# Half 0 of batch 0's tokens first in the planner's list, and a third scratch slot for narrowing

## The chip, the cores and the metric

One core of one Trainium2 chip. The time is device microseconds of one execution, the median of several runs. TensorE is PE below, VectorE DVE, ScalarE ACT, GpSimd POOL, and SyncE, which issues nearly all transfers, SP.

## What is computed

Nyström attention over 4 batches of 8 heads, 576 tokens and 64 columns per head, then two feed-forward layers over the 2304 tokens.

```python
def _attn_ref(q, k, v):
    m = 32                                   # landmarks: means of 18 tokens
    q_lm = q.reshape(B, H, m, S // m, D).mean(axis=3)
    k_lm = k.reshape(B, H, m, S // m, D).mean(axis=3)
    A, Bm, C = sm(q, k_lm), sm(q_lm, k_lm), sm(q_lm, k)
    Z = Bm.transpose(0, 1, 3, 2) / (norm1(Bm) * norm_inf(Bm) + 1e-06)
    for _ in range(6):
        Z = 2 * Z - Z @ Bm @ Z
    return (A @ Z @ C @ v)

def _moe_ref(x, w_gate, w_val, w_out, rms_g):          # 512 -> 1536 -> 512
    xn = x / np.sqrt(np.mean(x * x, axis=-1, keepdims=True) + 1e-06) * rms_g
    g = xn @ w_gate
    return (g * (1 / (1 + np.exp(-g))) * (xn @ w_val)) @ w_out

def _moe2_ref(x, w_in, w_out, s, b):                   # 512 -> 2048 -> 512
    r = np.maximum(x @ w_in, 0.0)
    return (s * (r * r) + b) @ w_out
```

All weights of the feed-forward layers arrive as 8-byte floats and are narrowed to 4 bytes on the chip.

## The kernel before

**Order.** No engine's order is written out by hand. Every step is put on a list as an operation with a key (when it is wanted), a cost on each engine that can do it, and the names it reads and writes. A planner (`Scheduler.run`) goes through time with those costs and issues, on the engine that is free first, the ready operation with the smallest key. Attention's keys come from `by_path`: the longer the way that is left, the smaller the key. Operations of a second part of batch 0, its last half of tokens, are in `batch_late` and get 2.0 added. The costs are the planner's own; they are no measured times. Where PE would stand early on, the planner puts in fillers (`warm`, L1746): products of ones that nobody reads.

**Batch 0's end.** The tokens of a batch are worked on in two halves of 288 (half 0 and half 1). For each half: x = A'(W) on PE (L1037), the squares on ACT (L1043), half of the squares' sum on DVE (L1048), the sum over partitions on PE (L1056, twelve small products), reciprocal on DVE (L1064, L1065), root on ACT (L1068), a diagonal on DVE (L1073), a broadcast by a product with ones on PE (L1078), two scalings of A' on DVE (L1084), and then each scaled tile is split into a rounded part (`xh`, ACT L1088) and a rest (`xl`, DVE L1090). The rounded part and the rest stand for a 4-byte number in products that take 1-pass operands. After both roots ACT loads another table for the tanh (L1071).

**Narrowing** (`narrow`, L1110 on). A block of 512 KB of 8-byte weights is loaded into a stage slot, ACT writes two scratch tiles from it, `ca` (L1145) and `cmag` (L1147, and L1155, or DVE with L1156), and DVE joins the two to 4-byte weights (L1159). There are two scratch slots of each kind, and three slots `rawg` for the narrowed gate and value weights and two, `rawo`, for the narrowed output weights. A narrowed block is stored too, for the later batches.

**Products.** Hidden columns are taken in 12 slices f = 0 to 11 of 128. For a slice: the gate and value weights are multiplied with batch 0's small matrix gw (`fused`, L1299, sixteen products into two banks), the result is split into `uh` (ACT L1311 or DVE L1312) and `ul` (DVE L1314), and then, for each half of tokens and for gate and value, six products (L1326) make one bank. ACT and DVE take it from there: tanh (L1343), a product (L1345), another (L1349). Four banks, 67 to 70, serve these products, the weight products and batch 1's attention by turns. From slice 0 on the output weights follow (L1372, L1390). Batch 1's attention is laid between by the planner: its transposes on PE are L613, in triples, and its copies L617 and L618.

## Time and profile before

| | |
|---|---|
| median of 3 runs | 829.31 us (828.41 to 831.85) |
| the profiled execution | 829.26 us, of which the span 827.5 us |
| PE busy | 810.5 us (98%) |
| DVE busy | 651.0 us (79%) |
| ACT busy | 531.4 us (64%) |
| POOL busy | 119.8 us (14%) |

Busy time of PE counts fillers and includes a modelled end of each product, so two products in a row overlap; the step from one start to the next is what a product costs. Time is counted from the start of the span. The rows on which the prediction rests are shown further down.

### The profile page before, as it was taken

To read this page: it belongs to the slowest core of one execution; us is meant where nothing else is said; L and a number is where in the kernel's file an instruction comes from. 1 tells how busy PE (TensorE), PEld (TensorE's weight loads), DVE (VectorE), ACT (ScalarE), POOL (GpSimd) and SP (SyncE) were. 2 spreads that over 40 slices of the span, in tenths; PEclk is the share of its full clock that TensorE was granted. 3 is DMA by queue.
4 is the path that set the end of the run, shared out by engine and by line. 5 is a ranking of instruction groups with operands and counts; after the bars stand their busy time and mean duration, and the time that the engine had idled before them with its cause. 6 is when DMAs were issued, how large, how long until landed. Compare 5 with 4: busy or idle time off the path is not lost.

```text
span 827.5 us, 16641 instructions
## 1 busy us (share of the span) xinstructions
PE 810.5 (98%) x6151; PEld 653.3 (79%) x6151; DVE 651.0 (79%) x1461; ACT 531.4 (64%) x1097; POOL 119.8 (14%) x173
## 2 busy tenths in 40 slices
PE   8899999999999999999999999999999999999997
PEld 5577767877787877888888888887888888888886
DVE  6888998777787777898998988799766767665554
ACT  5899987543534434688888976578555556565553
POOL 0370355117411132210100000000000000000000
PEclk9999999999999999999999999999999999999999
DMA  9999959652542313398978641232422432254234
GB/s 281 326 381 368 266 178 285 222 135 81 144 139 89 128 47 125 116 295 274 321 260 316 199 169 51 90 102 70 135 77 76 112 93 80 75 164 140 64 87 130
DMA packets 87234, 138.46 MB, mean 167 GB/s; under 512 B 26480, under 2 KB 49008, under 8 KB 87152
## 3 DMA queue, kind: packets, MB, share of 16 engines
q1 hardware_dynamic: 86960, 137.13, 52.3%
q8 instruction: 48, 0.79, 0.4%
q14 instruction: 34, 0.28, 0.1%
q10 hardware_dynamic: 192, 0.26, 0.1%
HBM read 114.82 MB, written 22.54 MB: 166 GB/s over the span
## 4 chain that ended last, share of the span: by engine, by line
PE 79%; DVE 11%; ACT 5%; DMA 2%; issue 2%; POOL 0%; DVEq 0%; SPq 0%; ACTq 0%; POOLq 0%
PE bank L1417 23%; PE bank L1282 17%; PE bank L1390 14%; PE bank L1326 14%; PE bank L1664 3%; PE bank L1299 3%; PE bank L754 1%; DVE w_all L1108 1%; DVE hl L1108 1%; DVE hbuf L1345 1%; PE bank L1372 1%; ACT ca_all L1145 1%; PE bank L675 1%; DMA stage<-in_moe_w_out_dram 1%; DVE rawg L1159 1%
## 5 line engine op out<-in xcount | busy, mean ns | idle before, releaser
L1417 PE MATMUL bank<-w_all,hh 128*128 128x512 f32 x472 | 148.0, 394 | 0.0
L1390 PE MATMUL bank<-hh,w_all 128*128 128x512 f32 (+1 forms) x448 | 144.6, 379 | 0.1
L1417 PEld LDWEIGHTS bank<-w_all,hh 128*128 128x128 f32 x472 | 88.2, 188 | 20.3
L1390 PEld LDWEIGHTS bank<-hh,w_all 128*128 128x128 f32 x448 | 81.6, 188 | 24.1 <-issue 9.5
L1417 PE MATMUL bank<-w_all,hl 128*128 128x512 f32 x236 | 93.1, 394 | 0.0
L1326 PE MATMUL bank<-xh,u_all 128*128 128x288 f32 x400 | 88.2, 300 | 0.5 <-DVE hbuf L1345 0.3
L1390 PE MATMUL bank<-hl,w_all 128*128 128x512 f32 (+1 forms) x224 | 83.0, 370 | 0.0
L1108 DVE TENSOR_TENSOR w_all<-rawo,w_all 128x512 fp32r<-128x512 f32 x86 | 62.1, 722 | 12.8 <-ACT w_all L1106 10.0
L1326 PEld LDWEIGHTS bank<-xh,u_all 128*128 128x128 f32 x400 | 66.2, 188 | 4.6 <-issue 1.0
L1343 ACT ACTIVATE hbuf<-bank 128x288 f32<-128x288 f32 x96 | 38.9, 405 | 32.4 <-PE bank L1326 30.2
L1326 PE MATMUL bank<-xl,u_all 128*128 128x288 f32 x200 | 59.0, 295 | 0.2 <-DVE xl L1090 0.2
L1326 PE MATMUL bank<-xh,xl 128*128 128x288 f32 x184 | 54.2, 295 | 0.0
L1326 PE MATMUL bank<-xl,xh 128*128 128x288 f32 x184 | 54.2, 294 | 0.0
L1417 PEld LDWEIGHTS bank<-w_all,hl 128*128 128x128 f32 x236 | 44.3, 188 | 10.6
L1345 DVE SCALAR_TENSOR_TENSOR hbuf<-hbuf,bank 128x288 f32<-128x288 f32 x96 | 42.5, 443 | 8.8 <-ACT hbuf L1343 8.3
L1106 ACT ACTIVATE w_all<-rawo 128x512 fp32r<-128x512 f32 x48 | 30.3, 631 | 28.7 <-PE bank L1390 14.6
L1390 PEld LDWEIGHTS bank<-hl,w_all 128*128 128x128 f32 x224 | 42.2, 188 | 5.5 <-DVE hl L1108 0.3
L1106 ACT ACTIVATE hh<-hbuf 128x288 fp32r<-128x288 f32 (+8 forms) x73 | 26.6, 389 | 21.9 <-PE bank L1390 13.9
L1585 ACT ACTIVATE xbuf<-xbuf,b_sb,s_sb 128x512 f32<-128x512 f32 (+1 forms) x34 | 26.0, 765 | 20.2 <-DVE xbuf L1596 19.7
L1155 ACT ACTIVATE cmag_all<-stage 128x512 f16<-128x512 f32 x48 | 37.9, 790 | 1.0
L1326 PEld LDWEIGHTS bank<-xl,u_all 128*128 128x128 f32 x200 | 37.6, 188 | 1.2 <-DVE xl L1090 0.4
L1108 DVE TENSOR_TENSOR hl<-hbuf,hh 128x512 fp32r<-128x512 f32 (+8 forms) x76 | 36.9, 495 | 1.6 <-ACT hh L1106 0.2
(316 smaller groups left out, 1940.3 us busy)
## 6 DMA issues: line engine op xcount, KB each, us to landing
rawg<-keptg SPq DMA_DIRECT2D x36, 512.0 KB, 4.4
stage<-in_moe_w_out_dram SPq DMA_DIRECT2D x28, 512.0 KB, 5.5
rawo<-kepto SPq DMA_DIRECT2D x48, 256.0 KB, 3.1
rawg<-kept SPq DMA_DIRECT2D x24, 512.0 KB, 3.6
rawo<-kept SPq DMA_DIRECT2D x36, 256.0 KB, 2.6
stage<-in_moe_w_in_dram SPq DMA_DIRECT2D x16, 512.0 KB, 5.4
keptg<-rawg SPq DMA_DIRECT2D x12, 512.0 KB, 6.1
kept<-tail SPq DMA_DIRECT2D x24, 256.0 KB, 3.7
```

The source lines that it names most:

```text
L1106: e.activation(out=hi(), in_=src(), func=ACTF.Copy) if e is nc.scalar
L1108: b = op({"dve": t_dve(n), "pool": t_pool(n)}, key, lambda e: e.tensor_tensor(out=lo(), in0=src(), in1=hi().bitcast(F32), op=ALU.subtract) ...
L1155: e.activation(out=upper(), in_=word(1).bitcast(F32), func=ACTF.Copy, scale=2.0 ** -100)
L1282: nc.tensor.matmul(out=ps.t, lhsT=a[h][:, 128 * kd:128 * kd + 128], rhs=x[kd][y].t, start=(first and kd == 0 and i == 0), stop=(last and k ...
L1299: nc.tensor.matmul(out=pU[g].t[m, 256 * j:256 * j + 256], lhsT=gw[b].t[p, m], rhs=r.t[p, :, 128 * k:128 * k + 128], start=True, stop=True)
L1326: nc.tensor.matmul(out=ps.t[:, 0:HC], lhsT=u[a].t[:, 256 * g + 128 * part:256 * g + 128 * part + 128], rhs=x[y].t.rearrange("p k n -> p (k ...
L1343: op(("act", t_act(HC)), tg, lambda e: e.activation(out=th.t[:, 0:HC], in_=pg.t[:, 0:HC], func=ACTF.Tanh, scale=0.5), r=[pg], w=[th])
L1345: op(("dve", t_dve(HC)), tg, lambda e: e.scalar_tensor_tensor(out=th.t[:, 0:HC], in0=th.t[:, 0:HC], scalar=1.0, in1=pg.t[:, 0:HC], op0=ALU ...
L1390: nc.tensor.matmul(out=A[c].t[:, 0:n], lhsT=w[a].t[:, 128 * c:128 * c + 128], rhs=hs[y].t[:, 0:n], start=(f == 0 and i == 0), stop=(f == F ...
L1417: nc.tensor.matmul(out=A[c].t, lhsT=hs[a].t[:, s], rhs=w.t[:, 512 * y:512 * y + 512], start=(f == 0 and i == 0), stop=(f == F2 - 1 and i = ...
L1585: e.activation(out=h.t[:, c:c + n], in_=h.t[:, c:c + n], func=ACTF.Identity, scale=s_sb, bias=b_sb) if e is nc.scalar
L1664: nc.tensor.matmul(out=ps.t[:, 0:n], lhsT=tot.t[:, 1024 * a + c:1024 * a + c + 128], rhs=xs[3, kd // 2][y].t[:, n * (kd % 2):n * (kd % 2) ...
```

## The change

Two things, both in batch 0's end. The operations of half 0 of batch 0 that make x (`chain`: those of the loop over the halves, from the product L1037 to the split L1090, for half 0) get 8 taken off their keys, so that they come ahead of others in the planner's list. And the first three slices' gate and value weights (`f < C_F`) may be narrowed in a third scratch slot: `rawo`'s first buffer serves as `ca`, its second as `cmag`. Until the last of these operations is planned (`free_c`) the two `rawo` buffers are held back from their own use.

```diff
--- before.py
+++ after.py
@@ -37,6 +37,8 @@
 SCORE = 0.26
 BMM = 0.15
 N_SUM = 2
+CHAIN = 8
+C_F = 3
 XB = 1
 SCORE2 = 1.02
 XC = 2.0
@@ -355,7 +357,13 @@
     ro_r = ring(2, [128, 512], "rawo")
     st_r = ring(3, [128, 512], "stage", I64)
     c_all = [sb.tile([128, 1024], d, name=f"{x}_all") for x, d in (("ca", F32), ("cmag", I32))]
-    ca_r, cm_r = (Ring([Slot(x[:, 512 * i:512 * i + 512]) for i in range(2)], True) for x in c_all)
+    c_two = [[Slot(x[:, 512 * i:512 * i + 512]) for i in range(2)] for x in c_all]
+    ca_r, cm_r = (Ring(x, True) for x in c_two)
+    c_more = [Slot(ro_r.slots[0].t), Slot(ro_r.slots[1].t.bitcast(I32))]
+    ca0_r, cm0_r = (Ring(x + [y], True) for x, y in zip(c_two, c_more))
+    c_ops = []
+    for x in ro_r.slots:
+        x.held = True
     u_all = sb.tile([128, 2048], F32R, name="u_all")
     u_r = [Ring([Slot(u_all[:, 1024 * x + 512 * i:1024 * x + 512 * i + 512]) for i in range(2)], True) for x in range(2)]
     w_all = sb.tile([128, 2048], F32R, name="w_all")
@@ -491,7 +499,7 @@
 
     xs, gw = {}, {}
     at_ops = []
-    batch_ops, batch_late = {}, {}
+    batch_ops, batch_late, chain = {}, {}, []
 
     def token(b, n):
 
@@ -1095,6 +1103,8 @@
                         out=mark, in_=part(1)[:, cols][:, 0:1].bitcast(F32)), r=wl, w=["sums"])
             if hf:
                 late.extend(mine[n_mine:])
+            elif first:
+                chain.extend(mine[n_mine:])
         batch_late[b] = late
 
 
@@ -1113,7 +1123,8 @@
         c = slice(128 * f, 128 * f + 128)
         wt = ((w_gate, w_val, w_out), (w_in2, None, w_out2))[kind - 1][part]
         rows = kind == 1 and part < 2
-        st, a, m = Buf(st0_r if rows else st_r), Buf(ca_r), Buf(cm_r)
+        early = rows and f < C_F
+        st, a, m = Buf(st0_r if rows else st_r), Buf(ca0_r if early else ca_r), Buf(cm0_r if early else cm_r)
 
         def wide(x):
             return x.rearrange("p (k f) -> p k f", k=KD) if rows else x
@@ -1161,6 +1172,8 @@
             op0=ALU.logical_shift_left, op1=ALU.bitwise_or), r=[a, m, *after], w=[w], pair=True)
         if rows:
             row_ops.extend(S_.ops[n_ops:])
+        if early:
+            c_ops.extend(S_.ops[n_ops + 1:])
         for o in S_.ops[n_ops + 1:]:
             o.after = RELC
 
@@ -1481,6 +1494,8 @@
     S_.by_path(batch_ops[0], -60.0, END0)
     for o in batch_late[0]:
         o.key += LATE
+    for o in chain:
+        o.key -= CHAIN
 
     def gate(name, ops, t, fn=lambda e: None):
         g = op(("pe", 0.0), t, fn, w=[name])
@@ -1521,6 +1536,10 @@
             e.dma_start(out=k[:, 768:1024], in_=d.t[:, 0:256])
 
         op(("sp", t_dma(256, 1 + f % 2)), key + 4, store, r=[d], w=[("k2", f)])
+
+    def free_c(_):
+        for x in ro_r.slots:
+            x.held, x.free = False, 0.0
 
     n_out = [0]
 
@@ -1543,6 +1562,8 @@
                     S_.by_path(batch_ops[b + 1], *at_time(b + 1))
                 else:
                     gate("attn", at_ops, t, free_w2)
+            if n == 2:
+                gate("c", c_ops, -1.0, free_c)
             u = us.pop((b, f))
             hidden(t, t + 0.85, b, f, 0, u)
             t += 2 * t_first
```

What the planner makes of it: the order differs from the first of these places up to about 148 us of the span before, and is the same from there on, apart from line numbers (L1043 is L1051 after the change, L1326 is L1339).

ACT, where batch 0's squares stand, before:

```order
L1155 ACTIVATE cmag_all<-stage_91 128x512
L1043 ACTIVATE region<-bank_64 128x288
...
L1043 ACTIVATE region<-bank_64 128x288
L1311 ACTIVATE u_all<-bank_69 128x256
L1145 ACTIVATE ca_all<-stage_92 128x512
L1147 ACTIVATE cmag_all<-stage_92 128x512
L1155 ACTIVATE cmag_all<-stage_92 128x512
L1068 ACTIVATE tail<-tail 96x3
L1145 ACTIVATE ca_all<-xbuf 128x512
L1147 ACTIVATE cmag_all<-xbuf 128x512
L1068 ACTIVATE tail<-tail 96x3
L1071 ACT_TABLE_LOAD
```

And with the change:

```order
L1166 ACTIVATE cmag_all<-stage_91 128x512
L1156 ACTIVATE rawo_88<-stage_92 128x512
L1158 ACTIVATE rawo_89<-stage_92 128x512
L1166 ACTIVATE rawo_89<-stage_92 128x512
L1051 ACTIVATE region<-bank_64 128x288
...
L1324 ACTIVATE u_all<-bank_69 128x256
L1156 ACTIVATE ca_all<-xbuf 128x512
L1158 ACTIVATE cmag_all<-xbuf 128x512
L1076 ACTIVATE tail<-tail 96x3
L1166 ACTIVATE cmag_all<-xbuf 128x512
...
L1076 ACTIVATE tail<-tail 96x3
L1096 ACTIVATE xh_81<-tail 128x288 x2
L1079 ACT_TABLE_LOAD
```

The narrowing of slice 1's gate weights (`stage_92`) has moved in front of the squares, and half 0's two copies (`xh_81`) in front of the table load; half 1's two stand behind it.

PE, from half 1's sum over partitions to the first hidden products, before (between the rows left out stand more fillers of the same kind, and behind them the other three groups of slice 0):

```order
L1056 MATMUL bank_68<-ones,region 96x1 x6
L1078 MATMUL bank_67<-xbuf,ones 128x288
...
L1078 MATMUL bank_63<-tail,ones 128x288
...
L1746 MATMUL bank_70<-ones 128x512
L1326 MATMUL bank_70<-xh_81,u_all 128x288
...
L613 MATMUL bank_70<-ident,region 128x128 x3
L613 MATMUL bank_69<-ident,region 128x128 x3
L613 MATMUL bank_70<-ident,region 128x128 x3
L613 MATMUL bank_69<-ident,region 128x128 x3
L1299 MATMUL bank_68<-rawg_86,gw_97 32x256
```

And with the change:

```order
L1064 MATMUL bank_68<-ones,region 96x1 x6
L1086 MATMUL bank_67<-xbuf,ones 128x288
L1312 MATMUL bank_70<-rawg_86,gw_97 32x256
...
L1312 MATMUL bank_69<-rawg_86,gw_97 32x256
L1086 MATMUL bank_63<-tail,ones 128x288
L1339 MATMUL bank_68<-xh_81,u_all 128x288
...
L1339 MATMUL bank_67<-xh_81,u_all 128x288
...
L1339 MATMUL bank_68<-xh_81,u_all 128x288
```

The weight product of slice 1 (`rawg_86`) has moved between the two broadcasts, into banks 70 and 69, and eight groups of hidden products follow in a row where four did; of the six triples of transposes before slice 3's weight product one is left, and ten fillers between the two broadcasts and the first hidden product are gone (two more stand ahead of half 1's sum).

ACT, at the roots of batch 1's two halves, before:

```order
L1068 ACT_TABLE_LOAD
L1068 ACTIVATE tail<-tail 96x3
L1147 ACTIVATE cmag_all<-stage_91 128x512
L1311 ACTIVATE u_all<-bank_70 128x256
L1068 ACTIVATE tail<-tail 96x3
...
L1343 ACT_TABLE_LOAD
L1343 ACTIVATE hbuf<-bank_68 128x288
```

And with the change:

```order
L1076 ACT_TABLE_LOAD
L1076 ACTIVATE tail<-tail 96x3
L1356 ACT_TABLE_LOAD
L1356 ACTIVATE hbuf<-bank_69 128x288
L1116 ACTIVATE hh_101<-xbuf 128x288
L1076 ACT_TABLE_LOAD
L1076 ACTIVATE tail<-tail 96x3
...
L1356 ACT_TABLE_LOAD
L1356 ACTIVATE hbuf<-bank_70 128x288
```

A tanh now stands between the two roots, with a table load on either side of it.

## Rows read from the trace of the kernel before

**Rows 1.** The page, busy time: engine, us, share of the span, instructions.

```profile
PE 810.5 (98%) x6151; PEld 653.3 (79%) x6151; DVE 651.0 (79%) x1461; ACT 531.4 (64%) x1097; POOL 119.8 (14%) x173
```

**Rows 2.** By stretches: us; busy PE, PEld, DVE, ACT, POOL; clock; DMA share, GB/s.

```profile
40.00:50.00 10.00, 7.88 (x73) 5.41 (x73) 8.62 (x17) 9.77 (x21) 9.50 (x12) 1.00 1.05 347
...
60.00:100.00 40.00, 39.45 (x463) 30.66 (x462) 35.26 (x100) 37.95 (x81) 5.38 (x6) 1.00 1.01 329
```

**Rows 3.** Timeline of ACT, 26 to 41 us: start, us, engine, line, operation [idle before].

```profile
27.32 0.78 ACT L1155 ACTIVATE cmag_all<-stage 128x512 f16<-128x512 f32 x1
30.64 2.53 ACT L1043 ACTIVATE region<-bank 128x288 f32<-128x288 f32 x8 [2.54 <-PE bank L1037]
...
33.25 0.75 ACT L1145 ACTIVATE ca_all<-stage 128x512 f32<-128x512 f32 x1
...
34.59 0.78 ACT L1155 ACTIVATE cmag_all<-stage 128x512 f16<-128x512 f32 x1
...
36.64 1.28 ACT L1071 ACT_TABLE_LOAD   x1
37.93 0.20 ACT L1071 ACTIVATE spare<-spare 128x1 f32<-128x1 f32 x1
38.04 0.76 ACT L1088 ACTIVATE xh<-tail 128x288 fp32r<-128x288 f32 x2
```

**Rows 4.** Timeline of DVE, 26 to 41 us.

```profile
30.46 0.68 DVE L1159 SCALAR_TENSOR_TENSOR rawg<-ca_all,cmag_all 128x512 int32<-128x512 int32 x1
31.99 0.76 DVE L1048 TENSOR_TENSOR region<-region 128x576 f32<-128x576 f32 x1 [0.85 <-ACT region L1043]
...
33.88 0.75 DVE L1048 TENSOR_TENSOR region<-region 128x576 f32<-128x576 f32 x1
34.55 0.15 DVE L1064 TENSOR_SCALAR tail<-bank 96x3 f32<-96x3 f32 x1
...
37.19 0.81 DVE L1084 TENSOR_TENSOR tail<-tail,bank 128x288 f32<-128x288 f32 x2
```

**Rows 5.** Timeline of PE, 26 to 41 us.

```profile
34.77 1.15 PE L1056 MATMUL bank<-ones,region 128*96 128x1 f32 x12
35.96 0.75 PE L1078 MATMUL bank<-xbuf,ones 96*128 96x288 f32 x2
...
37.33 0.75 PE L1078 MATMUL bank<-tail,ones 96*128 96x288 f32 x2
37.91 1.68 PE L1746 MATMUL bank<-ones 128*128 128x512 bf16 x7
39.24 0.48 PE L1326 MATMUL bank<-xh,u_all 128*128 128x288 f32 x1
```

**Rows 6.** Timeline of all engines from 36 us.

```profile
41.41 2.81 POOL L580 TENSOR_TENSOR region<-region 128x576 f32<-128x576 f32 x2
...
43.03 0.82 PE L613 MATMUL bank<-ident,region 128*128 128x128 f32 x6
...
43.15 2.76 DVE L1159 SCALAR_TENSOR_TENSOR rawg<-ca_all,cmag_all 128x512 int32<-128x512 int32 x2
...
46.33 1.22 PE L1299 MATMUL bank<-rawg,gw 64*32 64x256 f32 x16 [0.88 <-DVE hbuf L1345]
```

**Rows 7.** The chain of waits from 20 us, and PE's timeline from 56 us.

```profile
49.74 6.56 PE bank L1326 x48
...
56.23 0.66 PE L1299 MATMUL bank<-rawg,gw 64*32 64x256 f32 x16
```

**Rows 8.** Timelines of ACT and PE, 118 to 165 us.

```profile
125.16 0.38 ACT L1311 ACTIVATE xh<-bank 128x256 fp32r<-128x256 f32 x1 [1.19 <-PE bank L1299]
...
126.22 1.28 ACT L1343 ACT_TABLE_LOAD   x1
...
128.47 0.40 PE L1326 MATMUL bank<-xh,u_all 128*128 128x288 f32 x1 [0.34 <-DVE hbuf L1345]
...
137.60 0.68 ACT L1145 ACTIVATE ca_all<-stage 128x512 f32<-128x512 f32 x1 [3.14 <-DVE rawo L1159]
```

## What was predicted, with its working

> **What bounds the kernel now.** I read the page first: TensorE (PE) is busy for 98% of the span [rows 1], so time can be won only where PE stands, repeats fillers, or works on something that could wait. Next the busy time by stretches [rows 2]: between 40 and 50 us PE is busy 7.88 of 10 us, and between 60 and 100 us 39.45 of 40. ScalarE (ACT) is at 9.77 of 10 and 37.95 of 40 in the same stretches, and the granted clock is 1.00 (2.4 GHz) in both. So two engines are nearly full later on, and the loss sits in the start, where batch 0's attention ends and its first products begin. The rest I read in the timelines of single engines.
>
> Three things stand out. ACT is idle for 2.54 us before the squares of x at 30.64 [rows 3], with weights already loaded that it narrows only from 33.25 on. PE runs 7 fillers from 37.91 and starts the first hidden product (L1326) at 39.24 [rows 5]. And after the four products of slice 0 it has little to do: the weights of slice 1 are multiplied (L1299) at 46.33 after a wait of 0.88 us, and the next hidden products start at 49.7 [rows 6, 7]. I use the product of slice 3 with gw as a milestone, which both orders have and which stands at 56.23 now [rows 7].
>
> **The change, part by part.**
>
> *The third scratch slot.* ACT narrows slice 1's gate weights before the squares: three instructions that take 2.12 us now (33.25 to 34.59 + 0.78) [rows 3]. From 28.10 (27.32 + 0.78) they end by 30.2, inside the idle 2.54 us, so they cost nothing there and free 2.1 us later. VectorE's (DVE) joining step, 0.68 us, falls in the 0.85 us that it waits before 31.99 [rows 4], with about 0.1 us to spare. If that cover were gone, the square sums and the whole chain would start later by the excess. SyncE (SP) pulls slice 4's gate load in front of batch 1's second q load; q, v and one store move back by one issue and its 512 KB. They feed batch 1's first sums on GpSimd (POOL), which start at 41.41 [rows 6] and wait for batch 0's last x, so I take nothing; if v came late it would cost batch 1, not this stretch.
>
> *The first half of tokens first.* DVE does half 0's reciprocal as soon as u is done: at about 34.0 instead of 34.55, ahead of half 1's square sum of 0.67 us (33.88 to 34.55) [rows 4]. Half 1's sum then ends near 35.0, and its sum over partitions (L1056, 1.19 us from 34.77 to 35.96) [rows 5] runs to about 36.15. PE is in order, so half 0's broadcast (L1078) waits behind it and starts at 36.15, later than 35.96 now. Its result is there at 36.9 (0.75 for two; one alone can't take longer). DVE goes on at once with half 0's two scalings, where today the first starts at 37.19. So this step gains 0.3 us only: PE's order eats most of it.
>
> The ACT copies of half 0 start near 37.4, not 38.04, since the table load (1.28 us) [rows 3] now stands behind them. On PE slice 1's weights come next (0.66) [rows 7], then half 1's broadcast, which waits for DVE until 38.1 and takes 0.58 (37.33 to 37.91 today, when the fillers follow). The first hidden product starts at 38.7 against 39.24: 0.5 us, with slice 1's weights done.
>
> *What is late next.* Half 1's copies stand behind the table load and a spare activation, together 1.40 us (36.64 to 38.04) [rows 3]: 38.15 + 1.4 is 39.55, and two copies of 0.38 and two subtractions on DVE bring half 1's x to 41.0. Only two groups of products are ready before that. A group of six takes 0.82 us (48 in 6.56) [rows 7], so PE is done at 40.3. Two of the four banks hold slice 1's u, whose casts stand behind the tanh on ACT, and the third group needs a bank that DVE frees at about 42.0, after a joining step and one product step. PE waits 1.7 us: a new wait in place of the old. Then six groups, 4.9 us, to 46.9. Slice 2's weights need two banks back. DVE's joining steps meet POOL's additions here: two of them take 2.76 us at 43.15, beside POOL's 2.81 at 41.41 [rows 6], against 0.68 alone [rows 4]. I put the product between 47.1 and 47.7, its end between 47.8 and 48.4. Its u is cast behind slice 3's joining step and ready at 49.2 to 49.8; four groups, 3.3 us, bring the milestone to 52.5 to 53.1. That is 3.1 to 3.7 us before 56.23.
>
> But the old order had put six triples of batch 1's transposes (L613) into this stretch and the new one has one. Five are owed at 0.41 (0.82 for two) [rows 6], 2.05 us on an engine that has next to no room later [rows 2]. The net gain is 1.1 to 1.7, and I take 1.4. Both ends stay in the range. The outer bound: in the 21.46 us from 34.77 to 56.23 PE does 15.97 us of needed work (half 1's sum 1.19, two broadcasts 1.16, twelve groups 9.84, two weight products 1.32, six triples 2.46), so 5.5 us is all that could be won there. Below, the lead can shrink to nothing, since ACT is full for the next 40 us and owes copies of those transposes too.
>
> *Two more table loads.* Further on, batch 1's two roots no longer share one switch: the order has four loads where there were two. Today such a load takes 1.28 us at 126.22 [rows 8], so 2.56 us more on ACT. ACT stands 1.19 us at 125.16 and 3.14 us at 137.60 there [rows 8], which covers it in sum. What showed on PE of one switch today is the wait of 0.34 us at 128.47 for DVE behind the tanh [rows 8]. I take twice that, 0.7, as the nearest row; the ends are 0 and 2.56.
>
> The Trainium skill speaks against this part: "ScalarE: Activation LUTs", What ACT_TABLE_LOAD costs, gives some 2.66 us for every switch, a drain of 1.38 beside the load included. Here the trace differs: the spare activation begins 1.29 us after its load began and the copies at 1.40 [rows 3], so no such drain is seen. By the page the two loads would be 5.3 us, an estimate, and the sum 833.2 if all of it showed.
>
> **The sum.** The profiled execution took 829.26 us, with 827.5 of span; the median of the three runs is 829.31, so the profile stands for it. 829.26 - 1.4 + 0.7 = 828.56; I say 828.5.
>
> **Rivals.**
> *More of the stall goes.* If the casts of slice 1's u come before half 1's copies are missed, so that PE doesn't stand at 40.3 and 48, 2.7 us more are won: 828.5 - 2.7 = 825.8, and 824.5 where all of the 5.5 us are won (829.26 - 5.5 + 0.7). For it speaks that every engine's waits here are below 3 us; against it, that PE, ACT and DVE are each full by turns and the bank count is fixed.
> *Nothing lasts.* ACT, at 37.95 of 40 us [rows 2], paces the stretch to 100 us; it wins 2.1 us, waits some 0.7 for half 0's scalings where the table load now lies (36.64 to 37.4), and owes copies of the transposes. PE then catches up and waits later: 829.26 + 0.7 = 830.0.
> *The split switch ends last.* Between the two halves of batch 1, ACT does a root, a load, one tanh, a load, a root, a load. Each tanh frees one of four banks, so PE waits for each: with no lead left, 829.26 + 2.56 = 831.8, slower than before. It decides as soon as more than 1.4 us of the 2.56 lie in front of a product. Against it are ACT's 3.14 us of slack right behind.
> *It does nothing.* The order shows ACT writing the output weights' buffers and half 0's steps ahead, so this one is out.
>
> **How the numbers follow.** Forecast (827.3 to 829.7) 0.45; more of the stall goes 0.25, half of it below 825.2; nothing lasts 0.15; the split switch 0.15, half of it with further waits of batch 1's moved transposes behind it and above 833.4. About 0.5% (4.1 us) is what a measurement of this kernel can tell from no change. Faster than 825.2 has 0.12, slower than 833.4 has 0.08, the same 0.80. The range from 825.3 to 831.8 leaves out 0.12 below and some 0.08 above.
>
> **What would show it.** Right: in the timeline of the changed kernel ACT's narrowing in 28 to 30.2, with under 0.5 us of idle before the squares; the first hidden product near 38.7; slice 1's weight product near 37; PE idle 1 to 2 us from 40.3; the milestone at 52.5 to 53.1; four table loads near 115 to 127 and waits of PE there below 1 us. Wrong: squares later than 30.7 (the cover is gone), no idle of PE at 40 (then the gain is larger), a milestone later than 54.5, or a PE wait over 1 us behind a tanh near 125.

## The result, and the profile after

The changed kernel takes 835.88 us (median of 4, 835.41 to 837.21) and the kernel before, beside it, 829.07 (median of 4, 828.41 to 831.85). The ratio is 1.0067 with a 95% interval of 1.0051 to 1.0083: slower by more than half a per cent, and above the range that was given. The profiled execution is the longest of the four, 837.21 us with a span of 835.1, against 829.26 and 827.5 before. Line numbers of batch 0's end are 8 higher than in the kernel before (L1043 is L1051), and those of the products 13 higher (L1299 is L1312, L1326 is L1339, L1390 is L1403).

The page of the changed kernel, busy time and TensorE's clock in 40 slices of the span (tenths of full speed):

```profile
PE 818.2 (98%) x6143; PEld 659.7 (79%) x6143; DVE 650.7 (78%) x1457; ACT 534.9 (64%) x1100; POOL 123.1 (15%) x176
...
PEclk9899988999999999999999999999999999999999
```

PE is busy 7.7 us longer than in [rows 1] with 8 instructions fewer. So most of the loss in this execution isn't waiting: the same products take longer. The second line says why: the clock is below full speed in slice 2 (21 to 42 us) and in slices 6 and 7 (104 to 146 us). Cut finer, PE of the changed kernel by stretches (us; busy PE with instructions; granted clock; DMA share, GB/s):

```profile
36.00:38.00 2.00, 2.00 (x23) 0.66 1.17 294
38.00:40.00 2.00, 1.76 (x12) 0.50 1.02 197
40.00:42.00 2.00, 2.00 (x10) 0.50 1.07 229
42.00:44.00 2.00, 1.67 (x9) 0.64 1.00 319
44.00:116.00 72.00, 70.67 (x787) 1.00 0.98 316
116.00:118.00 2.00, 0.50 (x1) 1.00 0.86 344
118.00:120.00 2.00, 0.88 (x2) 0.64 0.08 25
120.00:126.00 6.00, 6.00 (x26) 0.50 0.39 134
126.00:132.00 6.00, 6.00 (x37) 0.50 0.44 159
132.00:140.00 8.00, 7.85 (x63) 0.99 0.71 208
```

A clock of 0.50 is the 1.2 GHz level, 1.00 the 2.4 GHz level. The clock falls to the lower one twice, near 37 (to about 43.4) and near 118.5 (to 132.2). In the profile of before the clock is 1.00 in every one of these stretches.

**The start.** ACT and PE of the changed kernel, from 28 us:

```profile
28.04 0.64 ACT L1156 ACTIVATE rawo<-stage 128x512 f32<-128x512 f32 x1
...
29.27 0.79 ACT L1166 ACTIVATE rawo<-stage 128x512 f16<-128x512 f32 x1
30.74 2.53 ACT L1051 ACTIVATE region<-bank 128x288 f32<-128x288 f32 x8 [0.68 <-PE bank L1045]
```

```profile
33.94 1.24 PE L1767 MATMUL bank<-ones 128*128 128x512 bf16 x5
35.27 1.15 PE L1064 MATMUL bank<-ones,region 128*96 128x1 f32 x12
...
37.20 1.10 PE L1312 MATMUL bank<-rawg,gw 64*32 64x256 f32 x16
...
39.25 0.85 PE L1339 MATMUL bank<-xh,u_all 128*128 128x288 f32 x1
...
43.09 0.56 PE L1339 MATMUL bank<-xh,u_all 128*128 128x288 f32 x1 [0.34 <-DVE hbuf L1358]
...
54.10 0.68 PE L1312 MATMUL bank<-rawg,gw 64*32 64x256 f32 x16
```

The narrowing went where it was meant to, inside ACT's idle time, and the squares start at 30.74 (30.64 in [rows 3]), released by PE and not by ACT. The seven fillers (L1767 here) that stood at 37.91 in [rows 5] are gone; so are the three at 36.55; the last ones run at 33.94, and behind them PE has one-column products, a broadcast and small products only. Slice 1's weight product takes 1.10 us; at full clock it takes 0.66 (e11 below). The wait for the third group has shrunk to 0.34 us since the slower products fill it. The milestone stands at 54.10, 2.13 us before that of [rows 7].

**The place that was not foreseen.** PE of the changed kernel, 115 to 121 us, then DVE, POOL, and DVE's cast of 128x224 in the view that groups by line and shape (busy us, mean ns):

```profile
115.19 0.77 PE L1027 MATMUL bank<-tail 32*64 32x288 f32 x16
117.31 0.50 PE L1403 MATMUL bank<-hh,w_all 128*128 128x512 f32 x1 [1.36 <-DVE hh L1117]
119.12 0.80 PE L1403 MATMUL bank<-hl,w_all 128*128 128x512 f32 x1 [1.30 <-DVE hl L1118]
...
120.14 0.45 PE L1339 MATMUL bank<-xh,u_all 128*128 128x288 f32 x1
120.38 0.45 PE L1339 MATMUL bank<-xl,u_all 128*128 128x288 f32 x1
```

```profile
115.09 2.17 DVE L1117 CAST hh<-xbuf 128x288 fp32r<-128x288 f32 x2
117.18 0.68 DVE L1170 SCALAR_TENSOR_TENSOR rawg<-ca_all,cmag_all 128x512 int32<-128x512 int32 x1
117.78 1.28 DVE L1118 TENSOR_TENSOR hl<-xbuf,hh 128x288 fp32r<-128x288 f32 x2
```

```profile
115.65 1.47 POOL L588 TENSOR_TENSOR region<-region 128x576 f32<-128x576 f32 x1
```

```profile
L1117 DVE CAST hh<-xbuf 128x224 fp32r<-128x224 f32 x1 | 1.5, 1475 | 0.0
```

Here output products (L1403) stand directly behind batch 1's small products L1027, while the hidden values that they multiply are still being split on DVE into `hh` and `hl`. PE does one product in the 3.2 us from 115.9 to 119.1, and the clock is 0.50 from about 118.5 to 132.2: a hidden product then takes a step of 0.24 us (120.14 to 120.38), where it takes 0.13 at full clock. In the kernel before the same split stood at 115.85, but three hidden groups, 18 products from 117.04, and other work stood on PE ahead of those output products, which ran at 122.32 without a wait. DVE and PE of the kernel before:

```profile
115.85 1.10 DVE L1107 CAST hh<-xbuf 128x288 fp32r<-128x288 f32 x2
```

```profile
122.32 0.50 PE L1390 MATMUL bank<-hh,w_all 128*128 128x512 f32 x1
```

PE's waits in 100 to 160 us, the changed kernel (total, times, longest): against this list before had none of L1390's at all.

```profile
PE bank L1403 <- DVE hl L1118: 2.4, 2, 1.3
PE bank L1403 <- DVE hh L1117: 1.4, 1, 1.4
```

**Where the time goes, summed.** From 30 us to the 14th weight product (156.91 before, 164.48 after) I added up PE's timeline: each row counts from its start to the next row's, less the idle time in brackets.

| us | waits | fillers | hidden products | output products | rest | all |
|---|---|---|---|---|---|---|
| before | 5.55 | 3.04 | 48.38 | 21.60 | 46.35 | 124.92 |
| after | 5.79 | 1.33 | 52.14 | 24.05 | 49.08 | 132.39 |

Waits and fillers together fell by 1.47 us. The products cost 8.94 more. Most of that lies in the two low stretches; about 1.1 us is there at full clock too (e9 below): the products L1372 as smaller pieces (14.48 to 15.07) and the attention's L736 (3.13 to 3.64).

### The profile page after: what moved, and what is told of

It is laid out like the page before. It is cut to its first block, busy times and chain, and to the rows that moved or that the text cites. A ratio compares the mean times of both kernels' runs of the same rounds, so it can differ in the third digit from the quotient of the medians.

```text
span 835.1 us, 16623 instructions
## 1 busy us (share of the span) xinstructions
PE 818.2 (98%) x6143; PEld 659.7 (79%) x6143; DVE 650.7 (78%) x1457; ACT 534.9 (64%) x1100; POOL 123.1 (15%) x176
## 4 chain that ended last, share of the span: by engine, by line
PE 75%; DVE 8%; ACT 3%; issue 1%; DMA 1%; SPq 0%; DVEq 0%; ACTq 0%
PE bank L1430 23%; PE bank L1295 17%; PE bank L1403 14%; PE bank L1339 13%; PE bank L1685 3%; PE bank L1312 2%; DVE hl L1118 1%; PE bank L762 1%; DVE w_all L1118 1%; DMA kept<-tail 1%; PE bank L683 1%; DVE hbuf L1358 1%; PE bank L1064 0%; DVE region L1118 0%; DVE hbuf L1362 0%
## 5 line engine op out<-in xcount | busy, mean ns | idle before, releaser
L1403 PE MATMUL bank<-hh,w_all 128*128 128x512 f32 (+1 forms) x448 | 146.3, 382 | 1.4 <-DVE hh L1117 1.4
L1403 PEld LDWEIGHTS bank<-hh,w_all 128*128 128x128 f32 x448 | 82.4, 189 | 26.4 <-issue 9.9
L1339 PE MATMUL bank<-xh,u_all 128*128 128x288 f32 x400 | 91.8, 309 | 0.6 <-DVE hbuf L1358 0.5
L1403 PE MATMUL bank<-hl,w_all 128*128 128x512 f32 (+1 forms) x224 | 83.8, 374 | 2.4 <-DVE hl L1118 2.4
L1339 PEld LDWEIGHTS bank<-xh,u_all 128*128 128x128 f32 x400 | 69.5, 196 | 5.6 <-DVE hbuf L1358 1.6
L1118 DVE TENSOR_TENSOR w_all<-rawo,w_all 128x512 fp32r<-128x512 f32 x84 | 59.0, 702 | 13.7 <-ACT w_all L1116 10.3
L1356 ACT ACTIVATE hbuf<-bank 128x288 f32<-128x288 f32 x96 | 38.7, 403 | 37.3 <-PE bank L1339 33.6
L1339 PE MATMUL bank<-xl,u_all 128*128 128x288 f32 x200 | 60.7, 303 | 0.0
L1339 PE MATMUL bank<-xh,xl 128*128 128x288 f32 x184 | 54.3, 295 | 0.3 <-DVE xl L1327 0.3
L1339 PE MATMUL bank<-xl,xh 128*128 128x288 f32 x184 | 54.2, 294 | 0.0
L1358 DVE SCALAR_TENSOR_TENSOR hbuf<-hbuf,bank 128x288 f32<-128x288 f32 x96 | 42.4, 441 | 9.2 <-ACT hbuf L1356 8.7
L1403 PEld LDWEIGHTS bank<-hl,w_all 128*128 128x128 f32 x224 | 42.6, 190 | 8.3 <-DVE hl L1118 3.1
L1116 ACT ACTIVATE hh<-hbuf 128x288 fp32r<-128x288 f32 (+9 forms) x73 | 26.7, 390 | 21.6 <-PE bank L1403 13.2
L1339 PEld LDWEIGHTS bank<-xl,u_all 128*128 128x128 f32 x200 | 39.4, 197 | 1.1
L1118 DVE TENSOR_TENSOR hl<-hbuf,hh 128x288 fp32r<-128x288 f32 (+8 forms) x77 | 38.8, 515 | 1.6 <-ACT hh L1116 0.2
```

The lines of the kernel that those rows point to most:

```text
L1116: e.activation(out=hi(), in_=src(), func=ACTF.Copy) if e is nc.scalar
L1118: b = op({"dve": t_dve(n), "pool": t_pool(n)}, key, lambda e: e.tensor_tensor(out=lo(), in0=src(), in1=hi().bitcast(F32), op=ALU.subtract) ...
L1339: nc.tensor.matmul(out=ps.t[:, 0:HC], lhsT=u[a].t[:, 256 * g + 128 * part:256 * g + 128 * part + 128], rhs=x[y].t.rearrange("p k n -> p (k ...
L1356: op(("act", t_act(HC)), tg, lambda e: e.activation(out=th.t[:, 0:HC], in_=pg.t[:, 0:HC], func=ACTF.Tanh, scale=0.5), r=[pg], w=[th])
L1358: op(("dve", t_dve(HC)), tg, lambda e: e.scalar_tensor_tensor(out=th.t[:, 0:HC], in0=th.t[:, 0:HC], scalar=1.0, in1=pg.t[:, 0:HC], op0=ALU ...
L1403: nc.tensor.matmul(out=A[c].t[:, 0:n], lhsT=w[a].t[:, 128 * c:128 * c + 128], rhs=hs[y].t[:, 0:n], start=(f == 0 and i == 0), stop=(f == F ...
```

## The experiments

How far each order is ahead or behind can be read at the k-th weight product (L1299 or its successor), which all have in the same order: its start less that of before, from PE's timelines. Behind the 14th the orders are alike, and what is lost by then stays lost; 0 to 2.1 us more come later, told at the end. The last column is the execution that was profiled; others of the same kernel can differ.

| | 4th (56.23) | 9th (103.46) | 14th (156.91) | clock in that profile |
|---|---|---|---|---|
| after | -2.13 | -1.21 | +7.57 | falls at 37 and 118 |
| e11, after again | -3.06 | -1.91 | +3.04 | falls at 119 |
| e1, before without fillers | +4.13 | +4.10 | +4.18 | falls at 38 and 52 |
| e2, after with fillers | -1.00 | +0.18 | +4.76 | falls at 37, full from 40 on |
| e3, third slot alone | -3.09 | -3.33 | -0.53 | full |
| e4, first half alone | -2.45 | +2.38 | +0.95 | full |
| e5, two output products later | -2.90 | -1.68 | +0.81 | falls at 39 |
| e6, more fillers | -1.81 | -0.66 | +3.89 | falls at 122 |
| e7, both | -1.81 | -0.66 | +0.77 | full |
| e9, both, five fillers | -2.57 | -1.42 | +1.12 | full |
| e16, after, short POOL | -1.59 | -0.84 | 0.00 | falls at 36 |

### Do the missing fillers cost the clock?

e1 takes ten fillers of batch 0's end out of the kernel before and leaves the rest of its order.

```diff
-WARM1 = 60.0
+WARM1 = 36.0
```

> The kernel before, with the ten filler products after the first three of the stretch 34 to 41 us left out (WARM1 36 instead of 60); they compute nothing, and the order of all else is the same. Theory A (the loss of the changed kernel begins with TensorE's clock: between 35 and 39 us only small products are left there and no fillers): the granted clock falls to about 0.5 for some us from about 37 on in this old order too, the hidden products at 39 to 43 take about 0.24 us each instead of 0.13, the fourth slice's weight product (L1299, 56.23 before) comes 1 to 3 us later, and the time is 830.5 to 833. Theory B (the fall of the clock there costs nothing, since the products wait for others anyway; all of the loss is the wait at 116 to 119 us): the time stays within 1.2 us of 829.1, whatever the clock does.

833.94 us (830.05 to 834.99, 10 runs) against 829.66; ratio 1.0038 (1.0023 to 1.0053). PE of e1 by stretches:

```profile
38.00:40.00 2.00, 1.51 (x4) 0.50 1.03 215
40.00:44.00 4.00, 4.00 (x18) 0.50 1.09 283
51.00:56.00 5.00, 4.56 (x32) 0.66 0.94 336
```

Without the ten fillers that I had counted as repeats, the clock falls near 38 and once more near 52, and the old order is 4.1 us late from the 4th weight product on, more than either theory had. In time it is 3.2 us by the ratio (1.9 to 4.4). The fillers don't rule a fall out: in the profile of e17 below, whose order has all of them and whose edit is felt only from 42 us on, PE shows

```profile
36.00:38.00 2.00, 2.00 (x7) 0.50 0.82 168
```

But all ten executions of e1 have a granted clock of 0.991 to 0.996, and of the 21 of the kernel before beside it 16 have 0.997 or more.

e2 gives the changed kernel fillers back (into any bank that is free, and three before slice 1's weight product; fifteen more run, the first at 37.0).

```diff
+MORE_AT = {49: 3}
...
+                for _ in range(MORE_AT.get(self.n_pe, 0)):
+                    warm(at)
...
-        if banks[7].held or banks[7].free + S_.CROSS > t:
+        x = next((x for x in reversed(banks) if not x.held and x.free + S_.CROSS <= t), None)
```

> The changed kernel with fillers put back: a filler may go to any free bank instead of the last one alone, and three more stand ahead of slice 1's weight product; all else in the same order. Theory A: granted clock 1.00 from 30 to 60 us; the fourth slice's weight product (54.10 in the changed kernel) at 51.5 to 53; of the 6.8 us lost some 1.5 to 3 come back, time 832.8 to 834.3, the rest lying at 116 to 132 us. Theory B (only the wait at 116 to 119 us and what follows it cost): the early part comes forward and the wait at 116 grows by as much; time 835 to 837, and the clock still 0.50 near 119 to 132.

835.15 us (834.0 to 841.57, 6 runs); ratio 1.0072 (1.0046 to 1.0099). The theory of the fillers alone missed: no gain. The clock still fell, from 36.6 to 40.0. PE's two waits for `hh` and `hl` stand as in the changed kernel (1.35 and 1.30 us), with one product between them, but here the clock doesn't fall behind them:

```profile
118.00:120.00 2.00, 0.50 (x1) 1.00 0.56 223
120.00:126.00 6.00, 5.51 (x55) 1.00 0.32 122
```

From the 9th to the 14th weight product e2 loses 4.58 us all the same. So the late wait costs by itself, without the clock; Theory B had the time right, and the clock of 0.50 near 119 to 132 wrong.

### Which part of the change?

e3 has the third slot alone (`CHAIN = 0`), e4 half 0's steps first alone (`C_F = 0`).

> The changed kernel with CHAIN 0: the third slot without the first half going first; its plan keeps seven fillers between 35 and 39 us. Theory A: granted clock 1.00 from 30 to 60 us, time 827.5 to 830.5 unless a wait of over 2 us stands elsewhere with a fallen clock behind it. Theory B (the third slot, by its moved instructions, makes the later stall): a wait of TensorE for a split of a hidden half, of over 1 us, between 105 and 130 us, and a time of 833 or more.

> The changed kernel with C_F 0: the first half goes first, without the third slot; its plan keeps five fillers between the two halves' spreading products. Theory A: granted clock 1.00 from 30 to 60 us, time 827.5 to 830.5 unless a wait of over 2 us stands elsewhere with a fallen clock behind it. Theory B (the order of the halves makes the later stall): a wait of TensorE for a split of a hidden half, of over 1 us, between 105 and 130 us, and a time of 833 or more.

e3: 833.35 (829.34 to 834.29, 6 runs), ratio 1.0043 (1.0027 to 1.006). Its executions at a granted clock of 0.999 took 829.34 and 829.40, those at 0.993 to 0.995 took 832.8 to 834.3. e4: 832.15 (830.74 to 833.52, 10 runs), ratio 1.0022 (1.0011 to 1.0034), at least 830.7 even with the clock at 1.00. Neither part alone wins. In e3 the lead is 3.3 us at the 9th weight product and 0.5 at the 14th. Summing PE between the two shows where it went: 2.7 us more of products, 1.18 of them L736, 0.90 L890, 0.53 L1078 and 0.35 L675. The attention's steps that before had done earlier were still owed. A lead at one milestone is worth only what isn't owed elsewhere.

### The wait near 117

e5 emits two output products of the changed kernel's PE order (the two that wait) some operations later; e6 keeps them in place and adds fillers, eight near 37 and whatever fits into free banks up to 60 us (twenty more in all); e7 does both; e8 adds fillers to the kernel before.

```diff
+            if e == "pe" and self.n_seen in (162, 167):
+                self.kept.append(o)
...
+                if self.n_seen == 170:
+                    for x in self.kept:
+                        x.fn(self.engines[e])
```

```diff
+MORE_AT = {46: 2, 48: 3, 49: 3}
```

> The changed kernel with two groups of three products of TensorE's order moved: the first two groups of the output product of slice 7 (L1403, the ones that wait 1.36 us for hh and 1.30 us for hl at 115.95 to 119.6) stand behind the three hidden groups, the spreading and the weight product that follow them; nothing else moves on any engine. Theory C (the changed order makes TensorE wait for a split that DVE does late, which costs by itself; the clock's falls come on top): no wait over 0.6 us between 112 and 122, granted clock 1.00 from 112 to 135, and 3 to 5 us come back: 830.5 to 833, the early fall at 36 to 43 remaining. Theory D (DVE bounds that stretch anyway, the wait only shows it): the idle time turns up again between 119 and 135 behind other work of DVE, and the time stays 834.5 to 836.5.

> The changed kernel with eight fillers more between 32 and 38 us (two ahead of the first one-column products, three ahead of the first half's spreading product, three ahead of slice 1's weight product) and the gaps after them filled in any free bank. Theory C: granted clock 1.00 from 30 to 60 us in the profile, hidden products 0.13 us each, the first at 39.5 to 40.2; of the loss 1 to 2.5 us come back, 833.3 to 835, the wait at 116 to 119 standing as before. Theory D (what is early does not count, since DVE bounds 110 to 135): 835 to 836.5. If the clock falls at 36.7 in spite of them, the fall is set by what stands before 36 us, and the fillers give nothing.

> The edits of the two runs before together: more fillers, and the two groups of slice 7's output product later. Theory C: granted clock above 0.997 and 828 to 830.5, what was predicted for the changed kernel. Theory D: 834 or more.

> The kernel before with fillers added in the same places as far as its order has them (two ahead of the first one-column products, three ahead of the first half's spreading product, gaps up to 60 us in any free bank). Theory C (the clock falls by chance in some executions of any of these kernels where TensorE has little work between 30 and 45 us): 828.8 to 829.6 with all granted clocks at 0.998 or more, so without the executions at 830.5 to 833 that the kernel before shows at 0.994 to 0.997. Theory D: no difference from before beyond the interval.

All four beside one kernel before at 830.31:

| | us (runs) | ratio, 95% |
|---|---|---|
| e5 | 831.94 (10) | 1.0021, 1.0010 to 1.0031 |
| e6 | 834.74 (5) | 1.0057, 1.0035 to 1.0079 |
| e7 | 832.08 (9) | 1.0033, 1.0019 to 1.0047 |
| e8 | 830.33 (10) | 1.0005, 0.9994 to 1.0015 |

PE by stretches, e6 first, then e7:

```profile
116.00:120.00 4.00, 1.33 (x18) 1.00 0.40 156
120.00:126.00 6.00, 6.00 (x36) 0.72 0.52 173
```

```profile
116.00:120.00 4.00, 3.06 (x38) 1.00 0.77 294
120.00:126.00 6.00, 4.94 (x42) 1.00 0.79 258
```

e6 and e7 differ by the two moved operations only. Left in their place they cost 2.7 us: with the wait, PE is busy 1.33 of 4 us and the clock is 0.72 behind it; without, 3.06 and 1.00. The clock is the smaller part of it: e6's two executions at 0.999 took 833.96 and 834.74, e7's seven at 0.999 and 1.00 831.89 to 832.94. DVE's cast of 128x224 is as long in e7 as in the changed kernel (1.48 us); there no output product stands behind it. e6 against the changed kernel shows what the fall near 37 costs in the new order: little (1.0057 against 1.0067, intervals that overlap), since slow products there fill waits, and twenty fillers take PE's time too. e8 shows that more fillers neither help nor harm the old order. And e7, with a clock of 1.00 throughout and no wait over 1 us, still takes 831.89 in its profiled execution: with both faults mended the new order doesn't win, and both theories on e7 missed.

e9 (both, with five fillers) asks whether the twenty fillers of e7 had eaten the gain.

```diff
+MORE_AT = {48: 2, 50: 3}
```

> The changed kernel with slice 7's two groups later (as in the fifth experiment) and five fillers more, two ahead of the first half's spreading product and three ahead of the second half's, where TensorE waited 0.68 us in the fifth. Theory E (with the wait at 116 and both falls of the clock gone, the new order is worth about what the old one is: TensorE's waits and fillers between 30 us and the join near 157 sum to about 7.5 to 8 us here against 8.6 before, and 1 us of that goes for products that run a little longer): clock 1.00 in the profile, the fourteenth weight product (L1299, 156.91 before) within 0.7 us of before, time 828.8 to 830.3. Theory F (something else in the new order costs 2 us or more): 831 to 832.5 with the clock at 0.999 or more.

833.6 (831.84 to 836.72, 4 runs); ratio 1.0058 (1.0035 to 1.0081). At a clock of 0.999 it took 831.84, as Theory F had it. The fillers had not eaten the gain: in the sum of PE's timeline waits and fillers are 6.18 + 2.51 = 8.69 us there, against 8.59 before. As fillers went, waits came.

e10 takes 2 off half 0's keys instead of 8.

```diff
-CHAIN = 8
+CHAIN = 2
```

> The changed kernel with one size changed: CHAIN 2 instead of 8. The planner then makes another order, which keeps ten fillers between 34 and 39 us and puts the output product of slice 7 behind two more hidden groups. Theory E (what the change costs is the clock and the wait, neither of which belongs to the idea of first half first): clock as often at 0.998 and more as in the kernel before, no wait over 1 us at L1403 between 105 and 130, time 828.5 to 830.5. Theory F (first half first costs by itself, as its run alone, at 832.15, suggests): 831.5 to 833.

830.87 (828.82 to 832.73, 10 runs) against 829.99; ratio 1.0014 (1.0003 to 1.0025), between the two theories. Its profile keeps ten fillers (three at 33.8, seven from 36.5) and has no wait of the output products over 0.4 us. The nearest to before, and not ahead of it. It has the one wait that the rival of the split switch spoke of: PE waits 1.66 us for the product step (L1358) on a bank whose tanh ACT starts at 127.22, behind the loads of 124.41 and 125.93:

```profile
128.17 0.40 PE L1339 MATMUL bank<-xh,u_all 128*128 128x288 f32 x1 [1.66 <-DVE hbuf L1358]
```

### The changed kernel again

e11 is the changed kernel, unaltered, once more.

> The changed kernel again, beside the two others on the same chip, with more executions: 835 to 837 where the clock is at 0.988 to 0.995. By theory E its time falls with the granted clock, about 0.8 us for each thousandth, and no execution comes near 830, since the wait at 116 us stands in all of them.

835.61 (833.12 to 837.65, 4 runs) against 829.99; ratio 1.0068 (1.0046 to 1.0090). Its profiled execution took 833.12, and the clock was 1.00 up to 118. So it shows the early mechanism without the first fall. PE of e11, and a stretch of it:

```profile
36.83 0.66 PE L1312 MATMUL bank<-rawg,gw 64*32 64x256 f32 x16
...
38.55 0.51 PE L1339 MATMUL bank<-xh,u_all 128*128 128x288 f32 x1
...
42.14 0.40 PE L1339 MATMUL bank<-xh,u_all 128*128 128x288 f32 x1 [1.64 <-DVE hbuf L1358]
...
47.23 1.22 PE L1312 MATMUL bank<-rawg,gw 64*32 64x256 f32 x16
...
53.17 0.91 PE L1312 MATMUL bank<-rawg,gw 64*32 64x256 f32 x16
```

```profile
120.00:126.00 6.00, 6.00 (x28) 0.51 0.47 166
```

The clock of the same program with the same order fell at 37 in one execution and not in the other; it fell in both behind the late wait, from 118.5 to 132.2 in one and from 119.0 to 125.8 in the other. What the second fall costs can be read between the 9th and the 14th weight product, where each of these orders has the same wait: e2 without a fall loses 4.58 us there, e6 with one of 3.4 us 4.55, e11 with one of 6.8 us 4.95, the first profile of the changed kernel with one of 13.7 us 8.78. Only the longest shows as a loss of its own.

### Who takes the lead between the 4th and the 14th product?

One theory was that DVE, or ACT, is too full there. e12 and e13 let DVE's joining step (L1159 before) write 64 of 512 columns from slice 6 on, in e9's order and in the old one; e14 and e15 cut ACT's two narrowing steps in the same way.

```diff
+        few = 64 if kind == 1 and f >= 6 else 512
...
-            out=dst().bitcast(I32), in0=a.t.bitcast(I32), scalar=3, in1=m.t,
+            out=dst().bitcast(I32)[:, 0:few], in0=a.t.bitcast(I32)[:, 0:few], scalar=3, in1=m.t[:, 0:few],
```

> The order of the ninth experiment (changed kernel, slice 7's two groups later, five fillers more), with VectorE's last step of the narrowing (L1170) done on 64 of 512 columns for the weights of slices 6 and up, so that the numbers of those weights are wrong; every instruction stays in its place. It takes some 18 x 0.6 = 10 us of work off VectorE between about 75 and 155 us. Theory G (the lead that the change wins by 56 us is lost because VectorE bounds the stretch up to 157): against the same cut in the kernel before, the fourteenth weight product comes 1 to 3 us earlier here. Theory H (the lead is lost in something else): it comes within 1 us of it or later, as in the ninth (+1.12).

> The kernel before with the same cut of VectorE's step (L1159 on 64 of 512 columns for slices 6 and up; the numbers of those weights are wrong). Theory G: its fourteenth weight product (156.91 before) comes 1 to 3 us earlier than without the cut, since VectorE bounds there. Theory H: it moves by less than 0.7 us.

> The order of the ninth experiment with ScalarE's first two steps of the narrowing (L1156 and L1158) on an eighth or a quarter of their columns for slices 6 and up (wrong numbers in those weights): some 36 x 0.5 = 18 us of work off ScalarE. If ScalarE is what bounds the stretch, the lead comes back here (1 to 3 us against the same cut in the kernel before); if VectorE is, it does not.

> The kernel before with the same cut of ScalarE's steps. If ScalarE bounds the stretch, the fourteenth weight product comes over 1 us earlier than 156.91; if not, within 0.7 us.

Against 830.26: e12 830.16 (ratio 0.9997, 0.9982 to 1.0012), e13 828.83 (0.9974, 0.9953 to 0.9995), e14 834.41 (1.0029, 0.9999 to 1.0059), e15 828.63 (0.9982, 0.9971 to 0.9993). From the 4th to the 14th product e9 loses 3.69 us and e12 2.07, a relief of 1.6; the old order gains 1.95 by the same cut (e13: +2.04 to +0.09, with falls of the clock near 27 and 37, ahead of the 4th). DVE's load is felt alike in both orders, so it isn't what the new order loses to. In e14's profile the clock fell three times. Its one execution at 1.00 took 830.13, 1.7 below e9's 831.84; the old order gains 1.6 by the same cut (e15 against 830.26). As far as one execution goes, ACT's load weighs alike in both orders too.

### Who makes DVE's split slow?

In the changed kernel the second cast took 1475 ns, beside POOL's sums of batch 1. e16 and e17 cut these sums (L588 and L592, 580 and 584 before) to 8 of 64 columns for batches 1 to 3, in the changed kernel and in the one before.

```diff
+            few = D if first else 8
...
-                out=y(), in0=x()[:, 0:9], in1=x()[:, 9:18], op=ALU.add),
+                out=y()[:, 0:9, 0:few], in0=x()[:, 0:9, 0:few], in1=x()[:, 9:18, 0:few], op=ALU.add),
```

> The changed kernel, all instructions in their places, with GpSimd's sums of the landmarks for batches 1 and up (L588, L592) on 8 of 64 columns, so that those sums are wrong. Theory I (the wait at 115.95 to 119.6 is there because VectorE's casts of hh and its subtraction for hl run beside GpSimd's sum: the casts took 0.77 and 1.48 us there against about 0.30 alone): the casts take about 0.3 us each, TensorE's waits at L1403 fall from 2.66 us to 0.6 to 1.4, the fall of the clock behind it becomes shorter or is gone, and the time falls by 1.5 to 4 us to 832 to 834. Theory J (VectorE is late for another reason): the casts stay near 1 us, the waits over 2 us, the time 835 to 837.

> The kernel before with the same cut of GpSimd's sums. Theory I: less than 1 us of gain, 828.5 to 830, since no product waits for a split that runs beside such a sum there (its hidden groups stand ahead of the output product). Theory J: as much gain as in the changed kernel.

e16: 829.66 (827.74 to 831.01, 10 runs) against 830.03, ratio 0.9988 (0.9977 to 0.9998). PE of e16, and its cast and the one of before (mean ns of one):

```profile
116.59 0.50 PE L1405 MATMUL bank<-hh,w_all 128*128 128x512 f32 x1 [0.28 <-DVE hh L1119]
117.92 0.50 PE L1405 MATMUL bank<-hl,w_all 128*128 128x512 f32 x1 [0.83 <-DVE hl L1120]
```

```profile
L1119 DVE CAST hh<-xbuf 128x224 fp32r<-128x224 f32 x1 | 0.4, 404 | 0.0
```

```profile
L1107 DVE CAST hh<-xbuf 128x224 fp32r<-128x224 f32 x1 | 0.9, 883 | 0.0
```

The waits are 1.11 us together instead of 2.66, and the clock stays at 1.00 behind them. The new order gains 6 us, more than either theory had. e17, the same cut in the old order: 827.57 (825.88 to 829.39, 7 runs), ratio 0.9966 (0.9953 to 0.9979), 2.5 us, where less than 1 was expected; POOL's sums cost the old order something too, which stayed unexplained. With the sums cut in both, the new order is 2.1 us behind the old one (829.66 against 827.57), about what e7 is behind it. What hangs on the meeting of POOL, split and output products in the new order alone is the difference, some 3.5 to 4 us. e5's move of two products came to the same size (835.61 to 835.88 without it, 831.94 with it).

The second cast begins at 115.78, behind POOL's sum (115.65), and ends at 117.26 (115.09 + 2.17), 0.14 us behind that sum's end (115.65 + 1.47 = 117.12). The same holds where POOL's instruction is another: the first cast of the changed kernel ends 0.17 us behind POOL's sum of 114.89, the second of the kernel before (883 ns) 0.13 behind one of 116.02, the second of e16 (404 ns) 0.14 behind one of 116.00. The one cast that began ahead of POOL's instruction, the first of before at 115.85, took 304 ns.

The Trainium skill, "SBUF — State Buffer", Two separate sides, says that VectorE and GpSimd share a pair of ports as an exclusive lock: of a VectorE operation in a two-port mode, or with two inputs in SBUF where GpSimd reads SBUF too, and a GpSimd operation, the one that starts first has the pair for its whole length, and the other stands. The trace agrees with that for each of these casts; in which mode they ran no row shows.

## Why the prediction was wrong

**Bounds, and the steps that failed.** I read waits and fillers of PE as the time to win and put the loss of before into its start. That is where it lay, and the change did reduce it, from 8.59 to 7.12 us up to the 14th weight product. Three steps of the sum failed.

- The net gain of 1.4 us. At full clock and with the late wait mended, the new order costs 1.8 us (e7 over before, medians; by the ratio 1.6 to 3.9). That is the largest error, 3.2 us.
- The far end of the order. The sum had 0.7 us for the table loads there and no term for the output products that moved up behind the split that feeds them. The loads cost nothing; the wait of 2.66 us for `hh` and `hl` stood in their place, and with the clock behind it costs 2.7 us (e6 over e7).
- The granted clock of 1.00 in [rows 2]. It depends on what PE does (e1), and was taken as given: no rival spoke of it, and the seven fillers of [rows 5], with three more, were dropped at no price. In the old order e1 prices the ten at 3 to 4 us; in the new order what is left for the fall near 37 is about 1 us, not told apart from the spread.

**The third slot.** As predicted: no cost, the cover of [rows 3] held. The squares came at 30.74, a trace behind the 30.7 named as the bound, with 0.68 us of idle before them (under 0.5 was named) that ended with PE's product, so the cover was not what set them.

**The first half first.** In e11, whose clock is full there, it came nearly to the tenth: weight product 36.83 (near 37), first hidden product 38.55 (38.7), a wait of 1.64 us that begins at 40.5 (1.7 from 40.3), slice 2's weights at 47.23 (47.1 to 47.7), the milestone 53.17 (52.5 to 53.1). In the profile of after the low clock put it to 54.10, and the wait at 40 vanished under slower products.

**The net gain of 1.4.** The lead was there, the work owed for it was mis-sized. Waits and fillers less what the smaller pieces cost more (1.1) leave 0.4 us in the profile of after; at full clock and with the late wait mended (e7, e9) the 14th product is 0.8 to 1.1 us late. e7 leads by 1.81 us at the 4th weight product. From there to the 14th its products take 3.30 us more than before's, not 2.05: the five triples of L613 cost 1.68, the smaller pieces of L1372 0.59, L736 0.51, and small differences the rest. Its waits are 0.72 shorter there, which gives the +0.77 of the table.

**Two more table loads.** They came, and cost nothing: ACT of the changed kernel

```profile
124.11 1.28 ACT L1076 ACT_TABLE_LOAD   x1
...
125.63 1.28 ACT L1356 ACT_TABLE_LOAD   x1
...
128.47 1.28 ACT L1076 ACT_TABLE_LOAD   x1
...
134.56 1.28 ACT L1356 ACT_TABLE_LOAD   x1
```

No PE wait behind a tanh there is above 0.3 us, though the low clock, which slows PE there, makes such waits less likely to show. e7 settles it: it has the same four loads at a clock of 1.00, and none of PE's waits of 0.3 us or more between 100 and 160 us is for a tanh or for the step behind it. The term was 0.7, and the ends 0 and 2.56 held it. In e10's order the split switch did cost PE 1.66 us.

**The rivals.** By its number "the split switch", 831.8, is nearest to what the mended orders do at full clock (831.9 and 831.8), and that is luck: no product of theirs waits behind a tanh near 125. "Nothing lasts", 830.0, has the better picture, a lead that is paid back, though not for the reason it gave: as far as e12 to e15 show, DVE's and ACT's load weigh alike in both orders. "The split switch" was looked for at 125 and the real place was 117: I had followed the moved table loads to PE and not the moved output products. The order showed the first output product of a new `hh` right behind L1027, without the hidden groups that had stood between, and the trace of before has its split on DVE at 115.85.

**The 5.6 us** that the comparison on one chip gives (e11, 835.61 against 829.99) fall into three parts: 1.8 the order itself with its fillers (e7 over before), 2.7 the late wait and the clock behind it (e6 over e7, which differ in that alone), and about 1.1 the first fall (the remainder). The first two are measured, on another chip than e11; the third is not told apart from the spread.

**What comes behind the 14th product.** e9 is 831.84 at a clock of 0.999, 2.6 us over before's profile, where the sum of its waits and fillers equals before's. The traces show most of it: 1.1 us by the 14th product, about 0.5 at 324 us, 0.4 between 420 and 455, and 0.3 outside the span. At 324 us DVE adds up squares (L1048) while POOL subtracts for `w_all` (L1108). In the kernel before DVE begins first, at 322.42, and its sum takes 0.76 us, POOL's step of 322.56 1.77. In e9, e7 and the changed kernel POOL begins 0.15 us ahead, its step takes 1.29 and DVE's sum 1.75, and PE waits 0.40 us for DVE. Between 420 and 455 us PE waits for DVE's splits by an amount that differs from execution to execution, from 0.4 us less than before to 1.5 more, in runs of the old order too (e8, e1); so it isn't the change.

**What stays open.** Why the same program's clock falls in one execution and not in the next, and why the same wait has a fall behind it in one and not in another (e2). Why POOL's sums cost the old order 2.5 us. And why 0.3 us more lie outside the span in the runs that have both parts of the change with CHAIN 8.

## What to carry to other kernels

A filler, or a dull stretch of PE, is not free to remove: before counting it as won, ask what PE does in the microseconds around it, and price the clock's fall as a rival with its own term (3 to 4 us in e1). When an edit to priorities moves work, follow the far end of the order too: look for products that now stand right behind the operation that makes their input, and read in the trace how long that operation takes beside its neighbours. A lead at a milestone counts only after what was postponed to get it.

## What the runs showed of the hardware

In the changed kernel's first profile the clock went to the 1.2 GHz level for 6.8 us (36.6 to 43.4) after five fillers, twelve one-column products and a broadcast, and for 13.7 us (118.5 to 132.2) after 3.2 us in which PE did one product; it rose again while PE ran products almost without a gap. It isn't the same in each execution: the same kernel had the first fall in one profile and not in the other, e2 had the same 3.2 us with one product and no fall, e17 fell at 35.4 with all the fillers in place, and the third slot alone took 829.3 us in one execution and 834.3 in another.

A cast of 128x224 on DVE took 404 ns beside a POOL instruction of 0.40 us, 883 beside one of 0.81 and 1475 beside one of 1.47; each ended 0.13 to 0.14 us behind POOL's. Which of the two engines began first decided who was slow: at 324 us a lead of 0.15 us of one or the other made DVE's sum 1.75 or 0.76 us, and POOL's step 1.29 or 1.77.
